# The inverse transform's turn through SBUF alone: four small transfers a frequency in place of a round trip through DRAM

## The chip, the cores and the metric

The kernel runs on one core of a Trainium2 chip. The metric is the device time of one execution in microseconds. The core has TensorE (matrix products), VectorE, ScalarE and GpSimd (arithmetic), SyncE (which here only issues DMA transfers) and 16 DMA engines that all transfers share. SBUF is the on-chip memory of 128 partitions, PSUM the memory that TensorE writes. In the profile PE is TensorE, PEld its weight loads, DVE VectorE, ACT ScalarE, POOL GpSimd, SP SyncE; a q behind the name is the engine's instruction queue.

## The reference

An input of 2048 positions and 512 channels goes through two branches that a gate mixes: a long convolution (state-space kernel, by a Fourier transform of twice the length) and a dense layer with a gelu.

```python
def _A_ref(u, A_re, A_im, B_re, B_im, C_re, C_im, log_dt, Dskip):
    dt = jnp.exp(log_dt)[:, None]
    ...
    P = jnp.exp(logdA[:, :, None] * l[None, None, :])
    K = jnp.einsum("dn,dnl,dn->dl", Cc, P, dB).real
    ...
    Yf = Uf * Kf                      # Uf, Kf: transforms of u and K padded to 2L
    y = irfft2(Yf)[..., :L] + u * Dskip
    ...
def _B_ref(x, w1, b1, w2, b2):
    h = gelu(x @ w1 + b1)
    return h @ w2 + b2

g = sigmoid((x * gate_w).sum(-1, keepdims=True))
return g * _A_ref(x, ...) + (1 - g) * _B_ref(x, ...)
```

All of it is float32: 2048 x 512 in, 2048 x 512 out.

## The kernel before

The kernel has two stages. The **front stage** (`front`) does the dense branch, builds the 2048 taps of the convolution kernel of each channel, and takes the first half of the forward transforms. Its work is a list of tasks (`Plan`); each has a cost, dependencies and a due time from the list `DUES`, and a planner orders them on every engine and queue. The first half of the transforms leaves the signal in DRAM as `tu_d` and the taps as `tk_d`, each 32 frequencies (`n`, 0 to 31) of 128 x 512 numbers, 256 KB a frequency. The dense branch's result, already scaled by one minus the gate, goes to `out` in DRAM.

The **convolution stage** (`conv`) follows in an order written out by hand. It is a loop of 16 steps `s`, two frequencies each. In a step TensorE does the second half of the signal's transform for the next step (`signal`, L1246, 8 matmuls by `pair`), that of the taps two steps ahead (`taps`, L1237, 8 matmuls), and the first half of the inverse for this step (`inverse`, L1265, 8 matmuls). ScalarE copies the taps' products from PSUM (L1243) and VectorE multiplies signal and taps (`product`, L1253). Each frequency's inverse is 128 rows of 512 in PSUM. Then comes the **turn** (`turn`, L1282): the second half of the inverse needs, for each position `q` of 32, a matrix whose 128 rows are the 32 frequencies times four parts, where the first half left the 32 positions of one frequency in different partitions. ScalarE copies a frequency from PSUM into one of six tiles `sa` (L1286), SyncE stores it into `t4_d` in DRAM (L1288, 256 KB), and when a group of eight frequencies is there, `quarter` (L1276) loads it back, eight positions at a time, into 32 partitions four apart. These loads go on GpSimd's queue for groups 0 and 1 and one of group 2, the others on SyncE's and ScalarE's at the end.

Positions 0 to 7 go into `den`, the others into `t3`. Both had another use before: `den` held the front stage's taps products (`xc`), then the signal of frequencies 0 to 7, which eight tasks of the front stage load into it (`early`, L519); `t3` held 16 of the frequencies' taps, fetched by `fetch` (L1209) on SyncE's queue. The signal's other frequencies lie in `attic` and `loft`, 11 and 8 rooms of 128 x 512, which the front stage fills too; the last five are loaded inside the loop (L1354) into rooms that have been read.

When the loop is done TensorE runs what is left of the dense branch (`rest`, L1315), and then the last half of the inverse: 16 row blocks (`pb`, L1390), two positions each, whose rows come from `den` or `t3`. VectorE scales each by the gate and adds it to the dense result (L1403), which `mix` (L1305) has loaded into freed rooms of `attic` and `loft`; SyncE and ScalarE store the sum.

Each DMA queue (SyncE's, ScalarE's, GpSimd's) issues in the order written; an issue waits for what its transfer reads and overwrites.

Of the kernel before, what the change touches and what calls it, by code (L numbers as in the profile page):

```python
# [57 lines left out]
T_EARLY, T_LOFT, T_DEN = 329.63, 507.38, 299.82  # L58
# [23 lines left out]
N_DEN = 8  # L82
N_ROOM = N_ATTIC + N_LOFT
N_US = N_DEN + N_ROOM
# [81 lines left out]

def seat(n, c, kind):

    return 4 * (16 * kind + 2 * (n % 8) + c) + n // 8
# [11 lines left out]
def constants():  # L181
# [41 lines left out]
    g2 = np.zeros((32, 64, 32, 2))  # L223
    for n, k in enumerate(ko):
        er, ei = om(4 * np.outer(q - 31.5, k + 32 * k1) + (q - 31.5)[:, None])
        f2[n, 0], f2[n, 1] = er, -ei
        a = 2.0 * np.pi * (k + 32 * k1 + 0.25) / L
        g2[n, :, :, 0] = np.cos(np.outer(a, m))
        g2[n, :, :, 1] = np.sin(np.outer(a, m))
        g2[n, :, 0, 1] = 1 - 2 * (k1 % 2)  # L230
# [121 lines left out]
def gated_mix(  # L352
# [21 lines left out]
    dr = ctx.enter_context(tc.tile_pool(name="dr", bufs=1, space=DRAM))  # L374

    dt_d = dr.tile([1, D], F32, name="dt_d")
    t4_d = dr.tile([4, 2, GROUP, 2, 32, D], F32, name="t4_d")
    tu_d = dr.tile([32, P, D], F32, name="tu_d")
    tk_d = dr.tile([32, P, D], F32, name="tk_d")

# [24 lines left out]
    def front(pool, psum, keep, attic, loft, den, pr):  # L405
# [113 lines left out]
        def early():  # L519
# [8 lines left out]
            for n in range(N_US):  # L528
# [3 lines left out]
                elif m < N_ATTIC:  # L532
                    due, key = T_EARLY + 2.5 * m, [keys[m]]
                else:
                    due, key = T_LOFT + m, ["xt", "xv"] if m < N_ATTIC + 4 else ["tt"]
# [955 lines left out]
```

## Time and profile before

| | |
|---|---|
| median of 3 runs | 501.41 us (500.95 to 503.88) |
| the profiled execution | 502.27 us |
| its span, first to last instruction | 500.4 us |
| TensorE, VectorE, ScalarE busy | 477.4, 428.1, 368.4 us |
| DMA moved | 107.56 MB in 81569 packets |
| HBM read and written | 61.14 and 45.62 MB |
| TensorE's granted clock | 0.999 |

The profile is of one execution, and its times are from the first instruction. A line "L1288" is line 1288 of the kernel before. A matmul's shape is partitions in * columns, and what it reads. In the chain of waits, each row is a piece of the path that ended last: its start, its length and what it was. The time to landing of a transfer runs from its issue until its completion is known.

### The profile page before, as it was taken

To read this page: it belongs to the slowest core of one execution; us is meant where nothing else is said; L and a number is where in the kernel's file an instruction comes from. 1 tells how busy PE (TensorE), PEld (TensorE's weight loads), DVE (VectorE), ACT (ScalarE), POOL (GpSimd) and SP (SyncE) were. 2 spreads that over 40 slices of the span, in tenths; PEclk is the share of its full clock that TensorE was granted. 3 is DMA by queue.
4 is the path that set the end of the run, shared out by engine and by line. 5 is a ranking of instruction groups with operands and counts; after the bars stand their busy time and mean duration, and the time that the engine had idled before them with its cause. 6 is when DMAs were issued, how large, how long until landed. Compare 5 with 4: busy or idle time off the path is not lost.

```text
span 500.4 us, 12185 instructions
## 1 busy us (share of the span) xinstructions
PE 477.4 (95%) x4802; PEld 354.1 (71%) x4802; DVE 428.1 (86%) x817; ACT 368.4 (74%) x632; POOL 38.3 (8%) x78
## 2 busy tenths in 40 slices
PE   8999999989999999899999989999899999999995
PEld 7899887778878878778887878887779522222451
DVE  4987999999999999999999999999940297877545
ACT  5999997999997789997867999647833466565310
POOL 2000000000000000001110020210100100231000
PEclk9999999999999999999999999999999999999999
DMA  8987587532768722745997234960486999989898
GB/s 299 307 288 279 189 249 236 170 97 74 220 168 243 224 85 88 236 145 131 203 241 265 85 53 128 168 134 3 152 250 156 244 390 384 359 315 390 295 335 316
DMA packets 81569, 107.56 MB, mean 215 GB/s; under 512 B 39284, under 2 KB 43784, under 8 KB 80968
## 3 DMA queue, kind: packets, MB, share of 16 engines
q1 hardware_dynamic: 74792, 82.80, 52.0%
q0 software_dynamic: 6016, 20.70, 15.6%
q10 hardware_dynamic: 704, 3.28, 1.8%
q8 instruction: 38, 0.62, 0.5%
q14 instruction: 19, 0.16, 0.1%
HBM read 61.14 MB, written 45.62 MB: 213 GB/s over the span
## 4 chain that ended last, share of the span: by engine, by line
PE 32%; DVE 31%; ACT 22%; issue 6%; DMA 6%; SPq 3%; POOL 0%; DVEq 0%; ACTq 0%; POOLq 0%
PE p2k L1235 5%; PE p2u L1235 5%; DVE loft L605 4%; DVE loft L604 4%; DVE y L780 4%; DVE y L765 3%; PE pa L1274 3%; ACT ph L1019 3%; DVE hl L1029 3%; ACT L1019 3%; PE ph L1002 2%; DVE phase L708 2%; PE ph L1004 2%; PE ph L1003 2%; DVE den L607 2%
## 5 line engine op out<-in xcount | busy, mean ns | idle before, releaser
L1002 PE MATMUL ph<-xh,wh 128*128 128x256 f32 x448 | 128.1, 286 | 3.3 <-DVE hl L1029 2.4
L1003 PE MATMUL ph<-xlo,wh 128*128 128x256 f32 x448 | 126.7, 283 | 0.0
L1004 PE MATMUL ph<-xh,wl 128*128 128x256 f32 x448 | 126.7, 283 | 0.0
L1002 PEld LDWEIGHTS ph<-xh,wh 128*128 128x128 f32 x448 | 85.1, 190 | 11.6 <-issue 3.9
L1045 PE MATMUL acc<-wh,hh 128*128 128x512 f32 x208 | 84.6, 407 | 2.7 <-ACT io L1070 1.2
L1003 PEld LDWEIGHTS ph<-xlo,wh 128*128 128x128 f32 x448 | 85.1, 190 | 1.9
L1048 PE MATMUL acc<-wh,hl 128*128 128x512 f32 x208 | 82.3, 396 | 3.6 <-DVE hl L1029 3.5
L1004 PEld LDWEIGHTS ph<-xh,wl 128*128 128x128 f32 x448 | 85.1, 190 | 0.0
L1046 PE MATMUL acc<-wl,hh 128*128 128x512 f32 x208 | 81.6, 392 | 0.0
L1019 ACT ACTIVATE ph<-ph,b1t 128x256 f32<-128x256 f32 x112 | 50.6, 451 | 21.8 <-PE ph L1004 19.9
L1045 PEld LDWEIGHTS acc<-wh,hh 128*128 128x128 f32 x208 | 39.1, 188 | 21.4 <-issue 7.3
L1029 DVE TENSOR_TENSOR hl<-ph,hh 128x512 fp32r<-128x512 f32 (+1 forms) x62 | 38.1, 615 | 18.5 <-PE acc L1046 9.3
L1048 PEld LDWEIGHTS acc<-wh,hl 128*128 128x128 f32 x208 | 39.0, 188 | 15.9 <-DVE hl L1029 7.5
L765 DVE TENSOR_TENSOR y<-y,ea 128x64 f32<-128x64 f32 (+4 forms) x80 | 45.2, 565 | 0.6
L1046 PEld LDWEIGHTS acc<-wl,hh 128*128 128x128 f32 x208 | 39.1, 188 | 6.1
L1243 ACT COPY k<-p2k 128x512 f32<-128x512 f32 x32 | 18.6, 586 | 26.7 <-issue 11.3
L780 DVE TENSOR_TENSOR y<-y,loft 128x2048 f32<-128x2048 f32 x16 | 36.6, 2285 | 0.8 <-ACT loft L728 0.6
L604 DVE TENSOR_TENSOR loft<-den,zz 128x256 f32<-128x256 f32 (+2 forms) x48 | 37.1, 772 | 0.1
L605 DVE TENSOR_TENSOR loft<-den,zz 128x256 f32<-128x256 f32 (+2 forms) x48 | 37.1, 772 | 0.1
L1022 ACT CAST hh<-ph 128x512 fp32r<-128x512 f32 (+1 forms) x62 | 32.9, 531 | 4.6 <-PE acc L1046 2.7
L805 PE MATMUL pk<-y,den 128*32 128x64 f32 x2048 | 35.0, 223 | 1.3 <-DVE y L791 1.1
L805 PEld LDWEIGHTS pk<-y,den 128*32 128x32 f32 x2048 | 31.8, 110 | 4.4 <-issue 2.2
(197 smaller groups left out, 882.0 us busy)
## 6 DMA issues: line engine op xcount, KB each, us to landing
tk_d<-sk SPq DMA_DIRECT2D x32, 256.0 KB, 5.1
t_d<-sa SPq DMA_DIRECT2D x32, 256.0 KB, 5.1
tu_d<-attic SPq DMA_DIRECT2D x40, 128.0 KB, 3.4
attic<-in_xt_dram SPq DMA_DIRECT2D x16, 256.0 KB, 3.8
attic<-in_xs_dram SPq DMA_DIRECT2D x16, 256.0 KB, 4.7
xl_d<-xlo SPq DMA_DIRECT2D x8, 512.0 KB, 6.2
xh_d<-xh SPq DMA_DIRECT2D x8, 512.0 KB, 4.6
out_dram<-io SPq DMA_DIRECT2D x16, 256.0 KB, 3.4
```

The source lines that it names most:

```text
L604: vec(2 * m, lambda: vv.tensor_mul(lines(t), lines(a), br), due, [ka, *kb], [kt])
L605: vec(2 * m, lambda: vv.tensor_mul(lines(v), lines(a), bi), due, [ka, *kb], [kv])
L765: nc.vector.tensor_mul(both(n, 64 - 3 * n, n), both(0, 64 - n, n), an)
L780: v.tensor_mul(y[:, 0].rearrange("p h (a b) l -> p h a (b l)", a=2), e.rearrange("p h (a b) l -> p h a (b l)", a=2), cc,)
L805: nc.tensor.matmul(pks[q][32 * j : 32 * j + 32, :, gg], x[:, r, ch // CL, :, ch % CL], y[:, r, ch // CL, :, ch % CL], start=(r == 0), stop ...
L1002: nc.tensor.matmul(p, h, xh[xk][:, d], start=(d == 0), stop=False)
L1003: nc.tensor.matmul(p, h, xlo[xk][:, d], start=False, stop=False)
L1004: nc.tensor.matmul(p, lo, xh[xk][:, d], start=False, stop=(d == 3))
L1019: nc.scalar.activation(phs[q][:, n], phs[q][:, n], AF.Gelu_apprx_tanh, bias=b1t[:, f : f + 1])
L1045: nc.tensor.matmul(a, h, wh[1][w], start=start, stop=False, skip_group_check=seeded)
L1046: nc.tensor.matmul(a, h, wl[1][w], start=False, stop=False, skip_group_check=seeded)
L1048: nc.tensor.matmul(a, l, wh[1][w], start=False, stop=stop, skip_group_check=seeded)
```

## The change

The DRAM tensor `t4_d` and `quarter` go. `turn` now issues, behind the copy of each frequency into `sa`, four transfers on SyncE's queue; each takes 32 partitions of `sa` (one of the four parts, 32 positions of 2 KB) and writes them one behind another into a single partition of `t3`, 64 KB. `home` gives the partition: the four parts of a frequency go four partitions apart, the two frequencies of a step 16 apart, and the next step's 64 away. The constants `g1` and `g2` are put in the matching order (`seat`, and parts before positions in `g2`), so that the products stay as they are.

`t3` grows from 24 to 32 rows and holds every position; `den` holds no positions any more. The taps' frequencies, which had `t3` and a pool of eight tiles, go in turn through the eight rows of `den`: eight are fetched ahead of the loop and two in each step. The signal no longer uses `den`: the eight tasks that loaded it are gone from the front stage with their eight due times (the other 1528 stay as they are, in their order), frequencies 0 to 18 go into the 19 rooms of `attic` and `loft`, and 13 instead of 5 are loaded inside the loop, on GpSimd's queue instead of SyncE's. All eight `mix` loads are on GpSimd's queue, at steps 6 to 13, into rooms given by `PAIRS`.

```diff
-T_EARLY, T_LOFT, T_DEN = 329.63, 507.38, 299.82
+T_EARLY, T_LOFT = 329.63, 507.38
...
-N_DEN = 8
-N_ROOM = N_ATTIC + N_LOFT
-N_US = N_DEN + N_ROOM
+N_US = N_ATTIC + N_LOFT
+PAIRS = (13, 15, 17, 0, 2, 4, 6, 8)
...
+def home(n):
+    return 16 * (n % 2) + 64 * (n // 2 % 2) + n // 4 % 4 + 32 * (n // 16)
+
 def seat(n, c, kind):
-    return 4 * (16 * kind + 2 * (n % 8) + c) + n // 8
+    return home(n) + 4 * (2 * c + kind)
...
-    g2 = np.zeros((32, 64, 32, 2))
+    g2 = np.zeros((32, 64, 2, 32))
...
-        return [den[:, k] for k in range(N_DEN)] + rooms + rooms[: 32 - N_US]
+        return rooms + rooms[: 32 - N_US]
...
             for n in range(N_US):
-                m = n - N_DEN
-                if m < 0:
-                    due, key = T_DEN + n, [("xc", n // 4)]
-                elif m < N_ATTIC:
-                    due, key = T_EARLY + 2.5 * m, [keys[m]]
+                if n < N_ATTIC:
+                    due, key = T_EARLY + 2.5 * n, [keys[n]]
...
         def fetch(n):
-            if N_TK <= n < N_TK + 16:
-                t2s[n] = t3[:, 16 + n - N_TK if n < N_TK + 8 else n - N_TK]
-            else:
-                t2s[n] = pool.tile([P, D], F32, tag="tk", name=f"tk{n}", bufs=N_TK)
+            t2s[n] = den[:, n % N_TK]
             nc.sync.dma_start(t2s[n], tk_d[ko[n]])
...
-        def quarter(on, g, h, n=8):
-            rows = t4_d[g].rearrange("e k c q d -> (e k c) q d")
-            to = t3[g:P:4, h - 8 : h - 8 + n] if h > 7 else den[g:P:4, h : h + n]
-            on.dma_start(to, rows[:, h : h + n])
         def turn(s):
             for n in (2 * s, 2 * s + 1):
                 sa = sas[n % 6]
                 nc.scalar.copy(sa, pas.pop(n))
-                g, k = divmod(n, GROUP)
-                nc.sync.dma_start(t4_d[g, :, k].rearrange("e c q d -> (c q) e d"), sa)
...
+                for j in range(4):
+                    at = home(n) + 4 * j
+                    nc.sync.dma_start(t3[at : at + 1], sa[32 * j : 32 * j + 32])
...
-        for n in range(N_TK, N_TK + 8):
-            fetch(n)
...
-            for n in range(16 + 4 * s, 20 + 4 * s) if s < 4 else ():
+            for n in range(2 * s + N_TK, min(2 * s + N_TK + 2, 32)):
                 fetch(n)
-            for n in range(2 * s + N_ROOM, min(2 * s + N_ROOM + 2, 32)) if s > 3 else ():
-                nc.sync.dma_start(us[n], tu_d[ko[n]])
+            for n in range(2 * s + N_US, min(2 * s + N_US + 2, 32)):
+                nc.gpsimd.dma_start(us[n], tu_d[ko[n]])
...
-            if 6 <= s < 13:
-                mix(s - 6, nc.gpsimd)
-            if s == 12:
-                quarter(nc.gpsimd, 2, 0)
+            if 6 <= s < 14:
+                mix(s - 6)
             turn(s)
...
-                        row = t3[:, j - 8] if j > 7 else den[:, j]
+                        row = t3[:, j]
```

More of the change, by code (lines that the diff above doesn't have):

```diff
@@ L227, in constants @@
         a = 2.0 * np.pi * (k + 32 * k1 + 0.25) / L
-        g2[n, :, :, 0] = np.cos(np.outer(a, m))
-        g2[n, :, :, 1] = np.sin(np.outer(a, m))
-        g2[n, :, 0, 1] = 1 - 2 * (k1 % 2)
+        g2[n, :, 0] = np.cos(np.outer(a, m))
+        g2[n, :, 1] = np.sin(np.outer(a, m))
+        g2[n, :, 1, 0] = 1 - 2 * (k1 % 2)
     f2 = f2.reshape(8, 4, P, 64).transpose(0, 2, 1, 3).reshape(8, P, 256)
@@ L376, in gated_mix @@
     dt_d = dr.tile([1, D], F32, name="dt_d")
-    t4_d = dr.tile([4, 2, GROUP, 2, 32, D], F32, name="t4_d")
     tu_d = dr.tile([32, P, D], F32, name="tu_d")
@@ L387, in gated_mix, with places @@
     c1t = cp.tile([P, 64], F32, name="c1t")
-    def places(attic, loft, den):
+    def places(attic, loft):
         rooms = [attic[:, k] for k in range(N_ATTIC)] + [loft[:, k * D : k * D + D] for k in range(N_LOFT)]
-        return [den[:, k] for k in range(N_DEN)] + rooms + rooms[: 32 - N_US]
+        return rooms + rooms[: 32 - N_US]
     def first(pr):
@@ L519, in early @@
         def early():
-            us = places(attic, loft, den)
+            us = places(attic, loft)
             keys = [("ux", 0)] + [("st", k) for k in range(3)]
@@ L528, in early @@
             for n in range(N_US):
-                m = n - N_DEN
-                if m < 0:
-                    due, key = T_DEN + n, [("xc", n // 4)]
-                elif m < N_ATTIC:
-                    due, key = T_EARLY + 2.5 * m, [keys[m]]
+                if n < N_ATTIC:
+                    due, key = T_EARLY + 2.5 * n, [keys[n]]
                 else:
-                    due, key = T_LOFT + m, ["xt", "xv"] if m < N_ATTIC + 4 else ["tt"]
+                    due, key = T_LOFT + n, ["xt", "xv"] if n < N_ATTIC + 4 else ["tt"]
                 move(
@@ L1199, in conv @@
         zs = [pool.tile([P, D], F32, name=f"z{k}", bufs=1) for k in range(2)]
-        us = places(attic, loft, den)
+        us = places(attic, loft)
         ko = k0_order()
@@ L1286, in turn, with mix @@
                 nc.scalar.copy(sa, pas.pop(n))
-                g, k = divmod(n, GROUP)
-                nc.sync.dma_start(t4_d[g, :, k].rearrange("e c q d -> (c q) e d"), sa)
-                if k < GROUP - 1:
-                    continue
-                if g == 3:
-                    for h in (8, 16):
-                        quarter(nc.sync, 2, h)
-                    for h, n in ((0, 4), (4, 4), (8, 8), (16, 8)):
-                        quarter(nc.scalar, g, h, n)
-                    quarter(nc.scalar, 2, 24)
-                    mix(7, nc.scalar)
-                    quarter(nc.scalar, g, 24)
-                elif g < 2:
-                    for h in (0, 8, 24) if g else (0, 8):
-                        quarter(nc.gpsimd, g, h)
+                for j in range(4):
+                    at = home(n) + 4 * j
+                    nc.sync.dma_start(t3[at : at + 1], sa[32 * j : 32 * j + 32])
         accs, mos = {}, {}
-        def mix(k, on):
-            r = 5 + 2 * k if k < 7 else 0
+        def mix(k):
+            r = PAIRS[k]
             if r < N_ATTIC:
@@ L1312, in mix @@
                 mos[k] = loft[:, r * D : (r + 2) * D].rearrange("p (s d) -> p s d", s=2)
-            on.dma_start(mos[k], out[2 * k : 2 * k + 2].rearrange("s p d -> p s d"))
+            nc.gpsimd.dma_start(mos[k], out[2 * k : 2 * k + 2].rearrange("s p d -> p s d"))
         def rest(n):
@@ L1334, in conv @@
             if n == 1:
-                t3 = pool.tile([P, 24, D], F32, name="t3", bufs=1)
+                t3 = pool.tile([P, 32, D], F32, name="t3", bufs=1)
                 g1t = pool.tile([P, 2, 64], F32, name="g1t", bufs=1)
-        for n in range(N_TK, N_TK + 8):
-            fetch(n)
         nc.sync.dma_start(g1t, g1.rearrange("p (b k) -> p b k", b=2))
@@ L1364, in conv @@
             inverse(s)
-            if s == 6:
-                quarter(nc.gpsimd, 0, 24)
-            if s == 10:
-                for g in range(2):
-                    quarter(nc.gpsimd, g, 16)
-            if 6 <= s < 13:
-                mix(s - 6, nc.gpsimd)
-            if s == 12:
-                quarter(nc.gpsimd, 2, 0)
+            if 6 <= s < 14:
+                mix(s - 6)
             turn(s)
@@ L1414, in gated_mix @@
     loft = keep.tile([P, 4160], F32, name="loft")
-    den = keep.tile([P, N_DEN, D], F32, name="den")
+    den = keep.tile([P, N_TK, D], F32, name="den")
     pr = keep.tile([P, 6, UW], F32, name="pr")
```

110 rows, old and new, of the table DUES are left out of this document.

## The prediction

> **What bounds the kernel now.** I read the page first, then the chain of waits over the last hundred microseconds, the busy time by stretch, SyncE's own timeline and the DMA view of single stretches. The page:
>
> ```profile
> span 500.4 us, 12185 instructions
> ...
> PE 477.4 (95%) x4802; PEld 354.1 (71%) x4802; DVE 428.1 (86%) x817; ACT 368.4 (74%) x632; POOL 38.3 (8%) x78
> ```
>
> TensorE is busy nearly always. The change rewrites the convolution stage, from about 392 us on. The chain of waits there:
>
> ```profile
> 392.39 6.11 DMA tk<-tk_d
> 398.50 0.04 issue
> ...
> 414.78 1.87 PE p2u L1235 x8
> 416.65 1.72 PE p2k L1235 x8
> 418.37 1.02 PE pa L1274 x8
> ...
> 470.60 1.02 PE pa L1274 x8
> ...
> 480.68 8.76 PE pb L1390 x40
> ```
>
> From about 402 to 489 us the chain holds nothing but matmuls. One step of the loop (signal, taps, inverse) is 1.87 + 1.72 + 1.02 = 4.61 us, so sixteen take 73.8 us. The last inverse ends at 471.62; the left-over dense products (`rest(16)`) fill the time until the final stage starts at 480.68, and they hide the last turn. By stretch:
>
> ```profile
> 402.00:472.00 70.00, 69.72 (x365) 20.09 (x364) 57.19 (x94) 38.72 (x73) 10.03 (x16) 1.00 0.97 358
> ```
>
> The columns after the length are TensorE, weight loads, VectorE, ScalarE and GpSimd busy, clock, DMA share and GB/s: TensorE 69.72 of 70 us, DMA engines 0.97 busy at 358 GB/s. So TensorE sets the pace, with the DMA engines just short of setting it.
>
> **What can be gained.** The change keeps every matmul, ScalarE copy and VectorE operation of this stage. What TensorE waited for at its start:
>
> ```profile
> 398.54 3.79 PE L1235 MATMUL p2k<-tk,pr 128*64 128x512 f32 x14 [0.19 <-DMA tk<-tk_d]
> 402.62 1.08 PE L1235 MATMUL p2k<-tk,cc 128*64 128x512 f32 x4 [0.28 <-ACT k L1243]
> ```
>
> That is 0.47 us, the most that earlier taps could give back. The eight loads taken from SyncE's list in the front stage, and the eleven that remain for `attic`, are these:
>
> ```profile
> L537 SPq DMA_DIRECT2D attic<-tu_d x11: 332/432/737, 264.8 to 269.8; - x11
> L537 SPq DMA_DIRECT2D den<-tu_d x8: 319/378/1338, 355.5 to 388.9; - x8
> ```
>
> Their eight issues of 0.38 us lie beside dense matmuls, and the signal's first rows now come from `attic`, whose loads are issued by 270 us: nothing on the path. The den tile is free for the taps before the taps' rows are in DRAM, because its last reader feeds those rows. At the far end, ScalarE loses its quarter loads and one mix load, and VectorE, which sets the pace of the last stretch, starts when the final products are ready:
>
> ```profile
> 481.74 1.61 DVE L1403 SCALAR_TENSOR_TENSOR attic<-pb,gate,attic 128x512 f32<-128x512 f32 x2 [11.52 <-PE pb L1390]
> ```
>
> It waited for TensorE, not for a mix load, so earlier mix loads give nothing. A gain is bounded by about half a microsecond. The question is only whether the new transfers stay hidden.
>
> **SyncE's queue, and how much it carries.** In the loop, SyncE now issues 24 taps fetches, 6 constants and 32 x 4 = 128 turns: 158 transfers; the 13 late signal loads and the 8 mix loads go on or stay on GpSimd's queue, where a signal load waits only for a product already issued and is used eight steps later, and a mix load is used after the loop: nothing on the path. How fast can SyncE issue?
>
> ```profile
> 392.01 1.86 SPq L1214 DMA_DIRECT2D tk<-tk_d  x4
> 393.91 0.43 SPq L1206 DMA_DIRECT2D cc<-in_c_dram  x1
> 394.38 3.09 SPq L1214 DMA_DIRECT2D tk<-tk_d  x4
> 398.57 5.36 SPq L1214 DMA_DIRECT2D t<-tk_d  x8
> 404.29 0.33 SPq L1339 DMA_DIRECT2D g1t<-in_g_dram  x1
> 404.96 0.33 SPq L1206 DMA_DIRECT2D cc<-in_c_dram  x1
> ```
>
> The chain showed one fetch, issued by 392.39, landing at 398.50. From that one (second of the first four) to the last of the second four, eight transfers go out; the ninth, into a tile nobody else uses, starts at 398.57, right behind that landing. So SyncE keeps at most eight transfers in flight, and a ninth waits for the landing of the one eight before it. The next eight take 5.36 us, 0.67 each. Under this limit the queue's pace is the time to landing over eight. The DMA view of the loop, 402 to 472 us:
>
> ```profile
> DMA packets 10873, 25.03 MB, mean 358 GB/s; under 512 B 1310, under 2 KB 2206, under 8 KB 10579
> ...
> t_d<-sa SPq DMA_DIRECT2D x30, 256.0 KB, 5.2
> ...
> t<-tk_d SPq DMA_DIRECT2D x11, 256.0 KB, 4.8
> tk<-tk_d SPq DMA_DIRECT2D x8, 256.0 KB, 5.5
> ```
>
> At 5.2 us a landing, 158 transfers need 158 x 5.2 / 8 = 102.7 us, against 73.8 us of matmuls. Before, the loop put only 59 on this queue (32 stores, 16 fetches, 5 signal loads, 6 constants), and it fitted.
>
> Is 5.2 us right for a transfer of 64 KB, a quarter of the size? From below: a lightly loaded 256 KB store, 128 partitions, window 102 to 107 us:
>
> ```profile
> q1 hardware_dynamic: 288, 0.52, 28.3%
> ...
> out_dram<-io SPq DMA_DIRECT2D x2, 256.0 KB, 2.1
> ```
>
> 0.52 MB is 256 packets of 2 KB; 28.3% of 16 engines over 5 us is 22.6 us, so 88 ns a packet. Eight packets an engine are 0.7 us; the other 1.4 us of the 2.1 are fixed. Now stores out of 64 partitions, window 90.5 to 93.5 us:
>
> ```profile
> q1 hardware_dynamic: 397, 0.66, 87.0%
> ...
> tu_d<-st SPq DMA_DIRECT2D x3, 128.0 KB, 3.6
> ```
>
> 0.66 MB is 322 such packets; 87.0% of 16 engines over 3 us is 41.8 us, so 130 ns a packet. [...]
>
> The new transfers read 32 partitions and write a single one, which no row shows. Bounds: if one partition took packets as fast as 128 do, 64 KB are two packets an engine, 0.18 us, and land in about 1.6 us. If it takes them one by one, 32 x 88 ns = 2.8 us, and 4.2 us to landing with nothing else about. A gain by the transfer itself is excluded, since the turn was hidden. I take the upper end, since halving the partitions already cost 1.5-fold and this goes from 128 to one. The four transfers of a frequency and the four of its partner go to eight partitions, four apart, and I let these run side by side. Between them queue the fetches (0.7 us an engine) and GpSimd's loads. The engines get no rest: 8.4 MB of turns, 24 x 0.26 of fetches, 13 x 0.26 of signal, 8 x 0.52 of mix and 6 x 0.20 of constants are 23.5 MB, as the loop's 25.03 before. So 4.2 us alone becomes the 5.2 us of the loop's rows.
>
> **Who waits.** Behind a turn held back on SyncE stand the fetches, two steps ahead of their taps products; behind the landing stands ScalarE's copy into one of six `sa` tiles, and behind that copy its next taps copies, then VectorE's products, then TensorE. The last landing holds the whole final stage, since every final product reads all frequencies.
>
> **The sum.** The loop's first issue is at 404.96. The 158th goes out 157 x 0.65 = 102.1 us later, at 507.1, and lands at 512.3. The final stage starts then and not at 480.68: +31.6 us. From there to the end the work is the same. The profiled execution took 502.27 us (span 500.4 and 1.87 around it), 0.86 above the median of 501.41. So 502.27 + 31.6 - 0.9 gives 533 us. With landings of 4.2 us the same sum gives 157 x 0.525 + 4.2 = 86.6, a start at 491.6, +10.9, 512 us; with 7 us, 157 x 0.875 + 7 = 144.4, +68.7, 570 us. Chance 0.52.
>
> **Rivals.**
>
> Not slower: the turns land fast. The queue's pace hides as long as 158 x landing / 8 is at most 73.8 us, that is up to 3.7 us; the 9.1 us from 471.62 to 480.68 cover the last landing. For it: 2.1 us in the quiet window, 1.6 us by the lower bound, smaller transfers. Against it: the full DMA engines and the 130 ns row. Then only the 0.47 us at the start change: 501 us. Chance 0.16. That something I don't see makes it over 1% faster: 0.03.
>
> SyncE's issuing sets the pace, not the landing. A turn before cost this much of the queue, a fetch this:
>
> ```profile
> L1288 SPq DMA_DIRECT2D t_d<-sa x32: 517/530/1375, 408.4 to 472.9; - x32
> ...
> L1214 SPq DMA_DIRECT2D t<-tk_d x16: 319/320/457, 398.6 to 411.8; - x16
> ```
>
> At 0.32 us 158 issues take 51 us and hide; at 0.53 they take 83.7, and with a landing of 2.1 the final stage starts at 490.8: +10, 511 us. Chance 0.08.
>
> Transfers to single partitions pile up. [...] Two at a time: 128 x 2.8 / 2 = 179 us and 24 x 0.7 = 17 us of fetches, final stage at 601 + 1.4, +122, 623 us; chance 0.14. Strictly one by one: 358 + 17 us, start at 781, +301, about 802 us; chance 0.07. [...]
>
> **The numbers.** Likeliest 533 us. About 1% (5 us) is what can be told from no change here. Slower: 0.52 + 0.08 + 0.14 + 0.07 = 0.81; within 1%: 0.16; faster: 0.03. The range goes from 500, which takes in the unchanged case, to 620, which leaves out the one-by-one case and the upper half of the two-at-a-time case: 0.07 + 0.07 + 0.03 left out. The likeliest case's own range is 512 to 570.
>
> **What would show it.** In the profile after: SyncE's timeline with turns close behind one another and waits on earlier turns' landings; turns landing in 4 to 7 us; a step of the chain at 6 to 7 us and not 4.61, with DMA or SyncE pieces between matmuls; ScalarE's `sa` copies waiting for DMAs; the final products starting near 512 us. The forecast is wrong if the chain still holds only matmuls from 402 to 489 us (turns under 3.7 us), or if turns land in 10 us or more with the engines busy and little moved (pile-up).

## The result, and the profile after

The changed kernel takes 613.32 us (median; 602.45 to 619.63) where the kernel before took 502.54 in the same comparison. Two of the four runs of the changed kernel (616.23 and 619.63 us) count as slow, and the other two (602.45 and 610.41) give 1.207 times as long, 95% interval 1.191 to 1.222, a loss of 104 us; by the medians it is 111. The prediction said 533 us and slower. The direction was right, and the median lies within the range of 500 to 620, but the loss is more than three times the 32 us that were forecast.

The profiled execution took 610.41 us. Its page, the lines that answer to those shown of before (section 1, the DMA and TensorE clock slices, and the chain by line):

```profile
span 608.7 us, 12293 instructions
...
PE 510.7 (84%) x4802; PEld 359.7 (59%) x4802; DVE 428.3 (70%) x817; ACT 368.7 (61%) x632; POOL 41.0 (7%) x83
...
PEclk9999999999999999999999999998778787887559
DMA  8976773356662647982557155889999999989937
...
DMA t<-sa 21%; DMA den<-tk_d 5%; DVE loft L603 4%; DVE y L763 3%; DVE loft L602 3%; DVE y L778 3%; PE ph L1000 2%; DVE hl L1027 2%; PE ph L1002 2%; PE ph L1001 2%; ACT ph L1017 2%; SPq L1278 2%; ACT L1017 2%; DVE phase L706 2%; PE acc L1046 2%
```

The turn (`t<-sa`) is now the largest item of the chain. TensorE's granted clock sinks in the last third of the span, to 0.78 from 402 to 587 us. The busy time by stretch, columns as in the prediction:

```profile
402.00:472.00 70.00, 45.99 (x169) 10.77 (x168) 30.43 (x50) 18.16 (x34) 6.25 (x11) 0.80 0.99 147
402.00:587.00 185.00, 109.67 (x399) 32.09 (x398) 56.23 (x92) 40.05 (x74) 10.59 (x17) 0.78 1.00 124
545.00:587.50 42.50, 8.34 (x37) 6.53 (x35) 0.00 (x0) 2.17 (x4) 0.00 (x0) 0.64 1.00 39
```

In the 70 us in which TensorE was busy for 69.72 before, it is busy for 45.99. The DMA engines are as full as before (0.99 against 0.97) and move 147 GB/s instead of 358. At the end, when nothing but turns is under way, they are full at 39 GB/s. In the chain of waits, turns stand where matmuls stood:

```profile
414.81 14.26 DMA den<-tk_d
429.06 0.04 issue
429.11 3.67 PE p2k L1230 x6
...
498.64 0.02 issue
498.65 0.51 SPq L1278
499.16 0.05 issue
499.21 0.58 SPq L1278
499.80 0.04 issue
499.84 8.73 DMA t<-sa
...
563.40 12.61 DMA t<-sa
576.01 0.02 issue
576.03 11.49 DMA t<-sa
587.52 0.24 issue
587.76 10.23 PE pb L1358 x40
```

The final products start at 587.76 and not at 480.68: +107.1 us, which is nearly all of the 108.3 by which the span grew. The rest is mostly their own length, 10.23 us for 40 matmuls instead of 8.76. The first turn is issued at 406.3 us, so the turns take 181.5 us to the start of the final products, 1.42 us each:

```profile
L1278 SPq DMA_DIRECT2D t<-sa x128: 502/536/2023, 406.3 to 576.0; - x128
```

The DMA view of 560 to 580 us, where only turns are in flight:

```profile
DMA packets 612, 0.84 MB, mean 42 GB/s; under 512 B 202, under 2 KB 202, under 8 KB 612
...
q1 hardware_dynamic: 612, 0.84, 113.7%
...
t<-sa SPq DMA_DIRECT2D x11, 64.0 KB, 12.6
```

0.84 MB are 12.8 transfers in 20 us, 1.56 us each. In the middle of the loop, where fetches and GpSimd's loads are under way too, they go out faster: 78 from 440 to 540 us, 1.28 us each. The 410 packets of 2 KB took 113.7% of 16 engines for 20 us, 887 ns each, against the 88 ns of the quiet store before.

### The profile page after: what moved, and what is told of

It reads as the page before. It is cut to its first block, busy times and chain, and to the rows that moved or that the text cites. A ratio compares the mean times of both kernels' runs of the same rounds, so it can differ in the third digit from the quotient of the medians.

```text
span 608.7 us, 12293 instructions
## 1 busy us (share of the span) xinstructions
PE 510.7 (84%) x4802; PEld 359.7 (59%) x4802; DVE 428.3 (70%) x817; ACT 368.7 (61%) x632; POOL 41.0 (7%) x83
## 4 chain that ended last, share of the span: by engine, by line
DMA 28%; DVE 27%; PE 19%; ACT 18%; issue 5%; SPq 3%; POOL 0%; DVEq 0%; ACTq 0%; POOLq 0%
DMA t<-sa 21%; DMA den<-tk_d 5%; DVE loft L603 4%; DVE y L763 3%; DVE loft L602 3%; DVE y L778 3%; PE ph L1000 2%; DVE hl L1027 2%; PE ph L1002 2%; PE ph L1001 2%; ACT ph L1017 2%; SPq L1278 2%; ACT L1017 2%; DVE phase L706 2%; PE acc L1046 2%
## 5 line engine op out<-in xcount | busy, mean ns | idle before, releaser
L1230 PE MATMUL p2k<-den,cc 128*64 128x512 f32 x56 | 40.0, 890 | 41.9 <-DMA den<-tk_d 38.9
L1252 DVE TENSOR_TENSOR v<-p2u,k 128x512 f32<-128x512 f32 x16 | 11.1, 691 | 89.8 <-ACT sa L1275 59.3
L1230 PEld LDWEIGHTS p2k<-den,cc 128*64 128x64 f32 x56 | 6.5, 167 | 66.9 <-issue 47.1
L1358 PE MATMUL pb<-t,g1t 128*64 128x512 f32 (+1 forms) x68 | 15.4, 614 | 34.4 <-DMA t<-sa 34.4
L1371 DVE SCALAR_TENSOR_TENSOR loft<-pb,gate,loft 128x512 f32<-128x512 f32 x6 | 4.2, 746 | 47.6 <-PE pb L1358 47.6
L603 DVE TENSOR_TENSOR loft<-den,zz 128x256 f32<-128x256 f32 (+2 forms) x48 | 37.2, 775 | 0.1
```

What stands on the lines that cost most here:

```text
L603: vec(2 * m, lambda: vv.tensor_mul(lines(v), lines(a), bi), due, [ka, *kb], [kv])
L1230: nc.tensor.matmul(out[64 * i : 64 * i + 64], w, x, start=True, stop=True)
```

## The experiments

The theory after the result, A: the single partition as the target limits a transfer into it, however many engines push, and the engines meet there (that they do is assumed; no view tells the engines apart). The rival, B: the number of transfers, on a queue that keeps eight in flight and needs half a microsecond for each issue (0.536 us in the median). Apart from the run with the turn through DRAM, each variant was run once.

**The transfers by themselves.** A kernel of nothing but groups of transfers; between groups VectorE adds one column of `t3` to `sa`, which waits for all of the group.

```diff
+    def lone(at, j):
+        nc.sync.dma_start(t3[at : at + 1], sa[32 * j : 32 * j + 32])
+    far = [16 * i + 4 * j for i in range(2) for j in range(4)]
+    near = [32 * i + j for i in range(2) for j in range(4)]
+    ...
+    for n in (1, 2, 4, 8):
+        for k in range(n):
+            lone(far[k], k % 4)
+        hold()
+    for n in (2, 4, 8):                  # the same with near
+    ...
+    for n in (1, 8):                     # 32 partitions into 32
+        nc.sync.dma_start(t3[js, k], sa[js])
+    ...
+    for n in (1, 8):                     # from DRAM into one
+        nc.sync.dma_start(t3[far[k] : far[k] + 1], xs[k + 1][0:32])
```

> The transfers by themselves, with nothing else on the chip; all of the reference's computation is left out, and what is stored is an input tile. Groups of 64 KB transfers, each group waited for: 1, 2, 4 and 8 from 32 partitions into one each, the targets four partitions or more apart as in the changed kernel; 2, 4 and 8 into neighbouring partitions; 1 and 8 from 32 partitions into 32; 1 and 8 from DRAM into one partition. Theory A (the 16 engines meet at the one target partition, and a transfer drains through it alone): one transfer lands in 3.5 to 4.5 us; in a group each further transfer into one partition adds 1.4 to 2.8 us, far apart or DRAM as the source alike, so eight take 14 to 24 us; eight into 32 partitions take under 7 us, set by the 0.5 us of an issue. Theory B (the count of transfers and the eight in flight, not the target): eight into one partition and eight into 32 partitions take the same, 5 to 7 us. Neighbours tell whether two partitions that lie together hinder each other more than two that lie apart: by A with a shared way into neighbours, 2.4 to 2.8 us for each further one; without, as far apart.

VectorE's timeline in this kernel, in the order of the groups (1, 2, 4, 8 far; 2, 4, 8 near; 1, 8 into 32 partitions; 1, 8 from DRAM). The time in brackets is its wait, which is the group's time from issue to the last landing:

```profile
22.25 0.21 DVE L382 TENSOR_TENSOR sa<-sa,t 128x32 f32<-128x32 f32 x1 [4.08 <-DMA t<-sa]
28.04 0.21 DVE L382 TENSOR_TENSOR sa<-sa,t 128x32 f32<-128x32 f32 x1 [5.58 <-DMA t<-sa]
37.05 0.21 DVE L382 TENSOR_TENSOR sa<-sa,t 128x32 f32<-128x32 f32 x1 [8.80 <-DMA t<-sa]
52.35 0.21 DVE L382 TENSOR_TENSOR sa<-sa,t 128x32 f32<-128x32 f32 x1 [15.09 <-DMA t<-sa]
58.98 0.21 DVE L382 TENSOR_TENSOR sa<-sa,t 128x32 f32<-128x32 f32 x1 [6.42 <-DMA t<-sa]
70.45 0.21 DVE L382 TENSOR_TENSOR sa<-sa,t 128x32 f32<-128x32 f32 x1 [11.26 <-DMA t<-sa]
91.74 0.21 DVE L382 TENSOR_TENSOR sa<-sa,t 128x32 f32<-128x32 f32 x1 [21.08 <-DMA t<-sa]
94.01 0.21 DVE L382 TENSOR_TENSOR sa<-sa,t 128x32 f32<-128x32 f32 x1 [2.06 <-DMA t<-sa]
100.88 0.21 DVE L382 TENSOR_TENSOR sa<-sa,t 128x32 f32<-128x32 f32 x1 [6.66 <-DMA t<-sa]
105.81 0.21 DVE L382 TENSOR_TENSOR sa<-sa,t 128x32 f32<-128x32 f32 x1 [4.72 <-DMA t<-in_xs_dram]
127.67 0.21 DVE L382 TENSOR_TENSOR sa<-sa,t 128x32 f32<-128x32 f32 x1 [21.65 <-DMA t<-in_xs_dram]
```

One transfer into one partition takes 4.08 us, into 32 partitions 2.06. Each further one adds (15.09 - 4.08) / 7 = 1.57 us far apart and (21.08 - 4.08) / 7 = 2.43 into neighbours, against (6.66 - 2.06) / 7 = 0.66 into 32 partitions, which is the issue (eight of that shape took 5.50 us to issue in the third kernel of transfers alone, 0.69 each). So the target sets the rate with nothing else on the chip, as A has it, and B falls for this part. The eight "near" targets are partitions 0 to 3 and 32 to 35; the second four add as much as the others, (21.08 - 11.26) / 4 = 2.46 us each, so transfers into partitions that lie together show no overlap, nor does the step from partition 3 to 32. A gives no reason for the 1.57 of targets that lie far apart. The last line has another cause than the first ones, seen in the DMA view of that group:

```profile
DMA packets 16, 0.52 MB, mean 24 GB/s; under 512 B 8, under 2 KB 8, under 8 KB 8
...
q1 hardware_dynamic: 16, 0.52, 5.9%
```

Eight of the 16 packets are under 512 B and the 0.52 MB are in the other eight, so each of the eight transfers is one packet of 64 KB. The packets took 5.9% of the time of 16 engines, and one engine is 6.25%, so on average no more than one engine was at work: 2.42 us for each further transfer (21.65 - 4.72 over 7). It does not bear on A.

**The same transfers into 32 partitions.**

```diff
-                    at = home(n) + 4 * j
-                    nc.sync.dma_start(t3[at : at + 1], sa[32 * j : 32 * j + 32])
+                    js = slice(32 * j, 32 * j + 32)
+                    nc.sync.dma_start(t3[js, n], sa[js])
```

> The changed kernel with its 128 turn transfers of 64 KB on the same queue, from the same 32 partitions, at the same places, but into 32 partitions instead of one; this leaves out the turn itself, the rest is computed on rows that weren't turned. Theory A (the single target partition): the turns land in 3 to 4 us and hide, 500 to 515 us in all. Theory B (158 transfers on a queue with eight in flight): landing stays at 8 us and the time near 613 us.

526.42 us beside 503.31 of the kernel before. With the single target partition 80 us of the loss go (87 by the medians); 23 stay, and the time lies above A's range of 500 to 515. The turns land in 3.2 us:

```profile
t<-sa SPq DMA_DIRECT2D x128, 64.0 KB, 3.2
```

SyncE's timeline of this kernel shows what is left:

```profile
413.01 7.60 SPq L1278 DMA_DIRECT2D t<-sa  x8
420.71 1.03 SPq L1209 DMA_DIRECT2D den<-tk_d  x2
421.83 4.95 SPq L1278 DMA_DIRECT2D t<-sa  x8
426.82 0.58 SPq L1204 DMA_DIRECT2D cc<-in_c_dram  x1
427.50 0.88 SPq L1209 DMA_DIRECT2D den<-tk_d  x2
428.47 6.54 SPq L1278 DMA_DIRECT2D t<-sa  x8
```

From 421.83 to 428.47 the queue issues without a pause: a step's eight turns, a constant and two fetches take 6.6 us, longer than the 4.61 us of its matmuls. In the groups of 7.60 and 6.54 us it also waits. The issues alone, 128 of 0.59 us, 24 fetches of 0.44 and six constants of 0.58, are an estimated 89 us, against the 73.8 us of the matmuls.

**One transfer a frequency.** The same kernel with the four transfers of a frequency in one.

```diff
-                for j in range(4):
-                    js = slice(32 * j, 32 * j + 32)
-                    nc.sync.dma_start(t3[js, n], sa[js])
+                nc.sync.dma_start(t3[:, n], sa)
```

> The run into 32 partitions again, with the four transfers of a frequency put into one of 128 partitions and 256 KB: 32 turn transfers on SyncE's queue instead of 128, the same bytes; the turn itself is left out as there. If that run's 24 us over the kernel before are SyncE's issues (128 of 0.59 us and 30 others are more than the 73.8 us of matmuls), they go: 500 to 506 us. If they are the DMA engines' load or the fetches' landing, they stay: 515 to 527 us.

502.76 us beside 502.57. With the same bytes in 32 transfers the 23 us are gone, so they are the price of the number of transfers; that it is their issuing is read from the timeline above. The change's other parts cost nothing in this kernel, whose loop has 316 GB/s on the DMA engines.

**Two queues.**

```diff
-                    nc.sync.dma_start(t3[at : at + 1], sa[32 * j : 32 * j + 32])
+                    (nc.sync, nc.scalar)[j % 2].dma_start(t3[at : at + 1], sa[32 * j : 32 * j + 32])
```

> The changed kernel with every second turn transfer on ScalarE's queue, so that 16 can be in flight and two queues issue. Theory A (a transfer drains through its target partition in 1.4 us whoever issued it): 128 x 1.4 = 180 us from the first turn as before, 595 to 620 us. Theory B (the queue's limit): 158 x 8.4 / 16 = 83 us from the first turn, 505 to 520 us.

648.91 us, slower than the changed kernel, and above the ranges of both theories. The turns did not drain faster from two queues (218.6 us from the first issue at 407.5 to the final products at 626.1, 1.71 us each, beside 1.42 in the changed kernel), so B falls for the whole kernel too. Why it got worse is not settled. Two waits by line (total, times, longest):

```profile
PE p2k L1230 <- ACT f L404: 87.4, 6, 18.6
ACT sa L1275 <- DMA t<-sa: 85.5, 12, 10.7
```

TensorE waits for ScalarE's constants `f`, which stand behind the turns that ScalarE now issues; it had no such wait in the changed kernel. The wait of ScalarE's `sa` copies for turns, 10.9 us in the changed kernel, is not the reason by itself: it is 90.5 us in the run with the fetches elsewhere (below), which is no slower. The fetches land later as well, 10.2 us in the median and not 7.6.

**Neighbours.**

```diff
 def home(n):
-    return 16 * (n % 2) + 64 * (n // 2 % 2) + n // 4 % 4 + 32 * (n // 16)
+    return 4 * n
...
-    return home(n) + 4 * (2 * c + kind)
+    return home(n) + 2 * c + kind
...
-                    at = home(n) + 4 * j
+                    at = home(n) + j
```

> The changed kernel with the four parts of a frequency in four neighbouring partitions instead of four that lie four apart; constants changed to match, all is computed. Theory A with a way into SBUF that neighbours share: no two of a frequency's transfers overlap, 128 x 2.4 to 2.8 = 307 to 358 us, in all 735 to 790 us. Theory A with each partition by itself the limit: as the changed kernel, 600 to 620 us. Theory B: the same 600 to 620 us.

722.03 us, below the range of A with a shared way (735 to 790) and far from the 600 to 620 of the others. First turn and final products:

```profile
L1278 SPq DMA_DIRECT2D t<-sa x128: 502/508/2227, 405.5 to 684.5; - x128
```
```profile
699.44 15.52 PE L1358 MATMUL pb<-t,g1t 128*64 128x512 f32 x68 [45.90 <-DMA t<-sa]
```

293.9 us for 128 turns, 2.30 each, close to the 2.43 us that neighbours took alone. The little that is missing may be overlap between one frequency and the next; no run tests that.

**Fetches off SyncE's queue.**

```diff
-            nc.sync.dma_start(t2s[n], tk_d[ko[n]])
+            (nc.sync if n < N_TK else nc.gpsimd).dma_start(t2s[n], tk_d[ko[n]])
```

> The changed kernel with the taps' 24 fetches of the loop on GpSimd's queue, so that they don't stand behind turns on SyncE's. Theory A (the turns drain at 1.4 us each whatever else is on the queue): 128 x 1.4 = 180 us from the first turn, 590 to 620 us. Rival (fetches that stand behind turns hold TensorE, and TensorE the next turns): 540 to 575 us.

605.51 us, inside what the changed kernel's own executions spread over. Fetches behind turns do not cause the loss. The 128 turns take 177.5 us from the first issue (404.4) to the final products (581.9), 1.39 us each, beside 1.42 in the changed kernel. The changed kernel took 1.28 us a turn in the middle of the loop and 1.56 at its end. So the rate for targets far apart is not a fixed one.

**The other parts of the change alone.** The turn goes through DRAM as before; taps in `den`, 32 rows in `t3`, signal and mix loads as in the changed kernel.

```diff
 def seat(n, c, kind):
-    return home(n) + 4 * (2 * c + kind)
+    return 4 * (16 * kind + 2 * (n % 8) + c) + n // 8
...
-                for j in range(4):
-                    at = home(n) + 4 * j
-                    nc.sync.dma_start(t3[at : at + 1], sa[32 * j : 32 * j + 32])
+                g, k = divmod(n, GROUP)
+                nc.sync.dma_start(t4_d[g, :, k].rearrange("e c q d -> (c q) e d"), sa)
+                ...                      # quarter as before, all into t3
```

> The changed kernel's other parts alone: taps through the eight rows of den, 32 rows in t3, the signal's 13 late loads and all mix loads on GpSimd's queue, but the turn through DRAM as before (stores of 256 KB, loads of eight positions into 32 partitions four apart). Theory A (all of the loss is the turn's transfers, by their target and by their number): 500 to 505 us, as the kernel before. Rival: the moved loads or the taps' short lead of two steps cost part of it, 510 to 525 us.

515.95 us, 1.027 times the kernel before (1.023 to 1.031): theory A's range for this kernel (500 to 505) is missed, the rival's (510 to 525) fits. Its chain of waits has fetches between the matmuls:

```profile
427.50 11.59 DMA den<-tk_d
439.13 3.24 PE p2k L1231 x6
...
451.54 12.15 DMA den<-tk_d
463.83 4.37 PE p2k L1231 x8
```

Beside the DRAM turn's 16.8 MB, these fetches take 12 us, and a lead of two steps (9.2 us) is too short. Before, with up to 16 fetches ahead of the loop, the same stores and loads hid. This is read from the chain; the lead was not changed by itself.

**What sets 1.57 us.** Two more kernels of transfers alone, each group of eight between waits as in the first.

```diff
+    both = [64 * (k % 2) + 4 * (k // 2) for k in range(8)]
+    half = [16 * i + 4 * j + 64 * i for i in range(2) for j in range(4)]
+    lone(far[k], 0)                      # one source for all
+    lone(both[k], k % 4)                 # targets alternate between the halves
+    lone(half[k], k % 4)                 # four low, four high
+    (nc.sync, nc.scalar)[k // 4].dma_start(...)
+    nc.gpsimd.dma_start(...)
+    nc.sync.dma_start(t3[far[k] : far[k] + 1, :, 0:256], sa[js, 0:256])
+    nc.sync.dma_start(t3[far[k] : far[k] + 1, 16 * i : 16 * i + 16], ...)   # 16 of these
```

> Again only transfers, everything else left out; groups of eight of 64 KB into one partition each, each group waited for. In the first such run eight far apart took 15.1 us (1.57 for each further one), eight into neighbours 21.1 (2.4), eight from DRAM 21.7 (2.4). Here: all eight from the same 32 partitions; targets alternating between the lower and the upper 64 partitions; four low, then four high; four on SyncE's queue and four on ScalarE's; all on GpSimd's queue; half as many bytes each (1 KB rows); and 16 of half the rows. Theory A (all 16 engines work the list in the same order and meet at one way into SBUF, 2.4 us a transfer, 1.57 because they drift apart a little): order and halves change little, 13 to 21 us; two queues let the engines work at two targets at once, 10 to 13 us; half the bytes take half of the increments, 8 to 10 us; 16 halves take what eight wholes take, 14 to 17 us. Theory C (the limit is in the SBUF source): the same source for all takes 2.4 us each, 20 us or more.

VectorE's waits, in that order, were 15.21, 15.08, 14.99, 15.16, 15.22, 7.41 and 12.34 us; the fourth, sixth and seventh:

```profile
79.26 0.21 DVE L382 TENSOR_TENSOR sa<-sa,t 128x32 f32<-128x32 f32 x1 [15.16 <-DMA t<-sa]
...
102.31 0.21 DVE L382 TENSOR_TENSOR sa<-sa,t 128x32 f32<-128x32 f32 x1 [7.41 <-DMA t<-sa]
...
114.86 0.21 DVE L382 TENSOR_TENSOR sa<-sa,t 128x32 f32<-128x32 f32 x1 [12.34 <-DMA t<-sa]
```

Source, half, order and queue change nothing, so theory C falls, and so does A's guess that two queues would let the engines work at two targets at once (10 to 13 us). The last two groups came out below A's ranges (8 to 10 and 14 to 17 us). They are near what SyncE takes to issue them (4.94 and 9.98 us) and a landing, so they show that half the bytes cost less, but not how much less.

```diff
+    for k in range(32):
+        lone(far[k % 8] + 32 * (k // 8 % 2) + 64 * (k // 16), k % 4)
+    nc.sync.dma_start(t3[far[k] : far[k] + 1, :, 0:256], xs[k + 1][0:32, 0:256])
+    nc.sync.dma_start(t3[far[k] : far[k] + 1, 0:16], xs[k + 1][0:32:2])
+    nc.sync.dma_start(t3[near[k] : near[k] + 1, :, 0:256], sa[js, 0:256])
+    nc.sync.dma_start(t3[far[k] : far[k] + 1].rearrange("o q (h d) -> o (q h) d", h=4), sa[:, 0:128])
+    nc.sync.dma_start(t3[js, k], sa[js])
```

> A third look at the transfers by themselves (everything else left out; each group waited for). Open is why 64 KB from SBUF into partitions far apart overlap in part (1.57 us for each further one) where 64 KB from DRAM don't (2.4 us, as neighbours). Groups: 32 transfers of 64 KB into 32 partitions that lie four or more apart, one group of eight after the other; eight of 32 KB from DRAM in 32 rows of 1 KB; eight of 32 KB from DRAM in 16 rows of 2 KB; eight of 32 KB into neighbours; eight of 64 KB out of all 128 partitions in rows of 512 bytes into one partition each; eight of 64 KB from 32 partitions into 32. Theory D (engines drift apart with the size and number of pieces each has per transfer): the 32 go on at 1.4 to 1.6 us each, 48 to 53 us; DRAM in small rows overlaps as SBUF does, 8 of 32 KB in 7 to 9 us; 128 partitions of small rows overlap at least as well as 32, 11 to 16 us. [...]

The waits were 52.61 us for the 32, then 7.75, 7.49, 11.23, 16.02 and 7.04.

```profile
70.78 0.21 DVE L382 TENSOR_TENSOR sa<-sa,t 128x32 f32<-128x32 f32 x1 [52.61 <-DMA t<-sa]
...
114.13 0.21 DVE L382 TENSOR_TENSOR sa<-sa,t 128x32 f32<-128x32 f32 x1 [16.02 <-DMA t<-sa]
```

The 32 go on at (52.61 - 4.08) / 31 = 1.57 us each, so the rate holds in this kernel beyond the first eight. DRAM in small rows overlaps as theory D had it: 7.5 us is near the 4.9 us of the issues and a landing, where half of the 2.42 us of the whole 64 KB for each further one, 1.2 us, would make over 11. So DRAM as the source does not by itself keep transfers from overlapping; in the first kernel each DRAM transfer was a single packet, with on average no more than one engine at work. The eight of 32 KB into neighbours took 11.23 us beside the 21.08 of 64 KB: half the bytes, about half the time. The 128 partitions of small rows, 16.02 us, are at the very end of D's range (11 to 16). D fits, but that the engines drift apart is not seen by itself. Why targets far apart get 1.57 us and not 2.43 / 2 or 2.43 / 8 is not settled by these runs, nor why the changed kernel reached 1.28 in the middle of its loop.

## Why the prediction was right and wrong

**What could be gained: right.** TensorE set the pace of the loop before, with 0.47 us to give back. With 32 whole transfers in place of the 128 into single partitions (and the turn itself left out) the kernel takes 502.76 us beside 502.57: the removed round trip through DRAM was hidden, and no gain from its removal can be told.

**A transfer alone: right, in part by luck.** 4.2 us were forecast and 4.08 measured. The part that depends on the target was put at 2.8 us and the fixed part at 1.4; neighbours show 2.43 for each further transfer, which leaves 1.65, so two small errors cancel. The expectations put a further neighbour at 2.4 to 2.8 us: 2.8 is the 32 x 88 ns of the prediction, and no run had shown the 2.4 when it was written. The runs showed 2.43 with the transfers alone and 2.30 a turn in the kernel with neighbours.

**The eight in flight: there, but not the bound.** SyncE does keep eight in flight, and turns wait for turns (35 times on its queue, 44.2 us in all). But the sum took the landing as the cause (5.2 us, so 0.65 us a transfer), while it is the consequence: eight in flight at 1.57 us each land in 12.6 us, the very number of the DMA view at the end. Over all turns the median landing was 8.4 us (the sum with it, 157 x 8.4 / 8 + 8.4, gives 173 us, near the 181.5 measured). Twice the queues did not help (648.91 us).

**The step that failed** is in the paragraph on 64 KB: the four transfers of a frequency and its partner "go to eight partitions, four apart, and I let these run side by side". They do so only in part: each adds 1.57 us alone on the chip and 1.42 in the kernel, where 0.65 was in the sum, and 0.66 is what the same transfers take into 32 partitions. The row of 130 ns for half the partitions was read in its direction only. With single partitions as targets a packet took ten times as long and not 1.5 times: 887 ns.

**The rival that came true** is the pile-up with two at a time, 128 x 2.8 / 2 = 179 us and 623 us in all, to which 0.14 was given: 181.5 us and 613. That the figures meet so closely is partly luck: a turn was put at 2.8 us and measured at 2.43, and the overlap was not two at a time throughout. By the 2.43 of neighbours an estimated 2.43 / 1.57, one and a half targets, were served at once with nothing else under way, and 2.43 / 1.28, nearly two, in the middle of the loop. No view tells the engines apart, so how they came to pile up is not shown. Of the signs named for a pile-up, full engines that move little are there (1.00 at 39 GB/s); landings of 10 us or more came only in part (13.3 us in the median from 410 to 430 us and 12.6 at the end, but 8.4 over all). The rival of one-by-one transfers (802 us) was nearest to the kernel with neighbours, 722.

**SyncE's issuing: right as a mechanism, too small.** 0.53 us an issue gave 83.7 us and +10; with targets of 32 partitions the kernel has 0.59 an issue (507/588 ns at the least and in the median) and loses 23. A step's queue took 6.6 us there without a pause, and more in the steps with waits for `sa` and landings. In the changed kernel this is mostly hidden under the pile-up: its chain has 2% of the span, some 12 us, on these issues.

**Nothing on the path for the moved loads: right in the changed kernel, not in general.** The chain after has no signal or mix load in it, and with 32 whole turns (502.76 us) they are free. The fetches are in that chain (5%), but on another queue they leave the time as it is. With the DRAM turn the same arrangement costs 13 us, by its chain through the fetches.

**Not foreseen:** TensorE's clock. It sank to 0.78 from 402 to 587 us. Over the 40 final products it was 0.86, where it had been 1.00 in the kernel before, and 8.76 / 0.86 are the 10.2 us that they took.

## What to carry to other kernels

Transfers of 64 KB into single partitions cost here 1.57 us for each further one with targets far apart, about the same from every queue tried (15.1 to 15.2 us for eight), and 2.43 into neighbours, against 0.66 into 32 partitions: before turning data by DMA into single partitions, time a few such transfers back to back, and not one alone. A transfer that the profile showed as hidden was worth nothing when it was removed (502.76 us beside 502.57), and its replacement has to fit the same cover in pace, which here was 4.61 us for eight transfers of 1.4 us. When transfers land late with a fixed number in flight, ask which rate makes them late: landing divided by the number in flight (12.6 us / 8 at the end of the changed kernel) was a result here and not the cause.

## What the runs showed of the hardware

- 64 KB from 32 partitions into one partition land in 4.08 us alone, into 32 partitions in 2.06. Back to back each further one costs 1.57 us with targets four or more partitions apart (41.7 GB/s), and 2.43 with the targets 0 to 3 and 32 to 35 (27.0 GB/s). In the changed kernel, with targets four or more apart, a turn took 1.28 us in the middle of the loop and 1.56 at the end; in the kernel with neighbours 2.30 over all. Queue, order, halves and source made no difference to eight far apart (14.99 to 15.22 us).
- Beside turns that piled up on SyncE's queue other transfers landed later, those of another queue too: GpSimd's 256 KB signal loads into `attic` in 12.1 us in the median and SyncE's fetches in 7.6, against 5.3 and 4.0 with the same turns into 32 partitions.
- 64 KB from one stretch of DRAM into one partition were a single packet, 2.42 us for each further transfer, with 5.9% of 16 engines busy; the same targets filled from DRAM rows of 1 or 2 KB overlapped (eight of 32 KB in 7.5 to 7.8 us, of which 4.9 to 5.0 are the issues).
- DMA engines read as full while they moved little: 1.00 busy at 39 GB/s, with 887 ns for a packet of 2 KB that took 88 elsewhere. In this case it was the target that slowed them: from 402 to 472 us they were 0.99 busy at 147 GB/s, and 0.81 busy at 235 GB/s with the same turns into 32 partitions.
- TensorE's granted clock was 0.78 from 402 to 587 us, with the engine 59% busy, 0.64 from 545 to 587.5 with 20%, and 1.00 in the loop of the kernel before with the engine full.
